# Row 35 of w2 as four eight-partition transfers in a gated attention and MLP decode step

## The chip, the cores and the metric

The kernel runs on one core of a Trainium2 chip. The metric is the device time of one execution in microseconds (us). Three runs of the kernel before gave a median of 721.89 us (721.79 to 722.36).

## The reference

All tensors are float32. Two tokens (B = 2) pass through an attention block with a cache and through an MLP, and a gate mixes the two.

```python
# D = 576, H = 32 heads, Dh = 128, Sk = 4096 cached positions, F = 4608
g = sigmoid((x * gate_w).sum(-1))                      # one gate per token
q = x @ wq                                             # [2, 32 heads, 128]
p = softmax(q . k_cache * Dh**-0.5)                    # over 4096 positions
a = (p . v_cache).reshape(2, 4096) @ wo                # wo: [4096, 576]
h = gelu(x @ w1 + b1)                                  # [2, 4608]
b = h @ w2 + b2                                        # w2: [4608, 576]
return g * a + (1 - g) * b
```

The caches hold 2 x 32 x 4096 x 128 values each, 134 MB each; w2 and wo hold 10.6 MB and 9.4 MB, wq and w1 9.4 MB and 10.6 MB. Everything is read once.

## The kernel before

**The ring.** A single tile `ring` of 128 partitions holds three slots of 64 KB per partition. At the start the slots hold wq and w1. Then come 16 items, each of four heads of one token: k of an item fills one slot, its v the next, and so on round the ring (`seq`, `load_heads`, line 130). At the end three loads called `last` bring w2 and wo (`LAST`, `load_last`, line 145). Weight rows are dealt so that partition p holds rows 36p to 36p+35 of w2 and rows 32p to 32p+31 of wo. "Row r" below means the r-th row of every partition: 128 rows of 576 values, 295 KB, over all the partitions. The three `last` loads hold 28, 28 and 12 such rows, each load cut into a few transfers.

**The queue.** All these transfers are issued by SyncE (SP), one after the other, in the order of the program. SP takes its instructions in order: one that waits holds all those behind it. The waits are not written in the kernel. The framework finds, for each transfer, which earlier instructions read or wrote the bytes that it overwrites, and puts a wait on the last of them in each engine. There are eight semaphores for SP's transfers, used in turn, so a transfer also waits for the transfer eight places ahead of it.

**Slots and their release.** The first `last` load goes into the slot of v of item 14, the second into that of k of item 15, the third into that of v of item 15. A v slot is released by the products of `av` (line 493, TensorE), a k slot by the reductions of `red` (lines 461 to 463: VectorE multiplies k by q in place at line 457, GpSimd folds a part in half, VectorE sums).

**The loop over items.** The step of item i does max and softmax of item i-1, multiplies and reduces k of item i on VectorE, then does the products with v of item i-1 on TensorE.

**The end.** After the loop, `mlp_out(0, 24)` multiplies rows 0 to 23 of w2 by h, `av(15)` follows, then normalization, interleaved with the remaining rows of w2, then rows 0 to 22 of wo into the accumulator `acc`, and rows 23 to 31 into `res` (`last_out`, line 415). The last row of wo comes in three pieces, so that little is left to do when the last one lands. `acc_mm(lhsT, rhs, k)` multiplies one row by two tokens: two products of 288 columns.

`hg` (line 384) is the gated h: hg[p, r, b] goes with row 36p + r of w2.

Of the kernel before, what the change touches and what calls it, by code (L numbers as in the profile page):

```python
# [8 lines left out]
F32 = mybir.dt.float32  # L9
AF = mybir.ActivationFunctionType  # L10
ALU = mybir.AluOpType
AX = mybir.AxisListType
P = 128
# [6 lines left out]
def kernel(  # L20
# [14 lines left out]
    nc = tc.nc  # L35
    B, H, SK, DH = k_cache.shape
    D = x.shape[-1]
# [20 lines left out]
    NF = F // P  # L58
# [5 lines left out]
    SLOTS = 3  # L64

    LAST = (
        (("w2", 0, 14), ("w2", 14, 28)),
        (("w2", 28, 36), ("wo", 0, 10), ("wo", 10, 20)),
        (("wo", 20, 23), ("wo", 23, 27), ("wo", 27, 30), ("wo", 30, 31), ("wo", 31, 32)),
    )  # L70
    FOLD = 23
    SLOT = R * DH
# [8 lines left out]
    cp = ctx.enter_context(tc.tile_pool(name="cp", bufs=1))  # L81
# [8 lines left out]
    ps_sm = ctx.enter_context(tc.tile_pool(name="ps_sm", bufs=3, space=bass.MemoryType.PSUM))  # L90
# [8 lines left out]
    kt, vt, wqt, w1t, rows = {}, {}, {}, {}, {}  # L99
# [22 lines left out]
    def slot(n):  # L122
        k = len(held) % SLOTS
        return ring[:, k * SLOT:k * SLOT + n]

    def load_heads(src, i):
# [3 lines left out]
        nc.sync.dma_start(t, src[i % B, h:h + E].rearrange("h (p r) d -> (h p) (r d)", p=PE_))  # L130
        return t.rearrange("p (r d) -> p r d", d=DH)

    srcs = {"w2": w2.rearrange("(p r) n -> p (r n)", r=NF), "wo": wo.rearrange("(p r) n -> p (r n)", r=32)}

    def load_last(m):
        n = sum(z - a for _, a, z in LAST[m]) * D

        used["e"], used["z"] = len(held) % SLOTS * SLOT + n, (len(held) % SLOTS + 1) * SLOT
        t = slot(n)
        o = 0  # L140
        for w, a, z in LAST[m]:

            ends = (a * D, a * D + DS, a * D + DS + DO, z * D) if (w, z) == ("wo", 32) else (a * D, z * D)
            for u, v in zip(ends, ends[1:]):
                nc.sync.dma_start(t[:, o:o + v - u], srcs[w][:, u:v])
                o += v - u
            for r in range(a, z):
                rows[w, r] = t[:, o - (z - r) * D:o - (z - r - 1) * D]

    def temp(n, parts=P):  # L150
        t = ring[:parts, used["t"]:used["t"] + n]
        used["t"] += n
        assert used["t"] <= SLOTS * SLOT
        return t
# [7 lines left out]
    def load():  # L162
        if not seq:
            return
        kind, i = seq.pop()
        if kind == "wq":
            wqt[i] = load_w(wq, ROWS[kind], i)
        elif kind == "w1":
            w1t[i] = load_w(w1, ROWS[kind], i)
        elif kind == "k":  # L170
            kt[i] = load_heads(k_cache, i)
        elif kind == "v":
            vt[i] = load_heads(v_cache, i)
        else:
            load_last(i)
        if kind in ("k", "v", "last"):
            held.append((kind, i))
# [28 lines left out]
    ident = cp.tile([P, P], F32, name="ident")  # L206
# [12 lines left out]
    for j in range(NPB):  # L219
        t = cp.tile([P, NT * EB + 32 - EB], F32, name=f"p{j}")  # L220
# [121 lines left out]
    def acc_mm(lhsT, rhs, k, start=False, stop=False):  # L342
        m = lhsT.shape[-1]
        for s in range(NS):
            o = 64 * (k % 2) + 32 * s
            nc.tensor.matmul(  # L346
                acc[o:o + m], lhsT, rhs[:, s * DS:(s + 1) * DS], start=start, stop=stop, skip_group_check=True
            )
# [27 lines left out]
    hg = cp.tile([P, NF, B], F32, name="hg")  # L376
    t = temp(NF * B).rearrange("p (r b) -> p r b", b=B)
# [6 lines left out]
    nc.vector.tensor_mul(hg, t, g1.unsqueeze(1).to_broadcast([P, NF, B]))  # L384
    load()

    def mlp_out(lo, hi):
        for r in range(lo, hi):
            acc_mm(hg[:, r], rows["w2", r], r)
# [6 lines left out]
    def o_turn(turn):  # L396
        t = late(B * 32).rearrange("p (b c) -> p b c", c=32)
        for b in range(B):
            nc.vector.transpose(t[:, b], oT[:, b])
        ps = ps_sm.tile([P, B * 32], F32, tag="sm", name="op_t")  # L400
        nc.tensor.matmul(ps, turn, t.rearrange("p b c -> p (b c)"), start=True, stop=True)
        nc.vector.tensor_copy(oP.rearrange("p b c -> p (b c)"), ps)

    def wo_out(lo, hi):
        for r in range(lo, hi):
            acc_mm(oP[:, :, r], rows["wo", r], r)
# [110 lines left out]
    def norm_sum():  # L517
        sums = ps_sm.tile([NO, 1], F32, tag="sm", name="psum")
        nc.tensor.matmul(sums, rs, ones, start=True, stop=True)
        f = late(1, NO)  # L520
        nc.vector.reciprocal(f, sums)
        nc.vector.tensor_mul(f, f, gall)
        nc.vector.tensor_reduce(osum, oall.rearrange("p (r d) -> p d r", d=DH), AX.X, ALU.add)
        nc.vector.tensor_scalar_mul(osum, osum, f[:, 0:1])

    def norm_t():
        ps = ps_sm.tile([P, NO], F32, tag="sm", name="oT_t")
        nc.tensor.transpose(ps, osum, ident[:NO, :NO])
        nc.vector.tensor_copy(
            oT.rearrange("p b (h e) -> p h b e", e=E), ps.rearrange("p (h b e) -> p h b e", b=B, e=E)  # L530
        )
# [22 lines left out]
    max_n(k)  # L554
    softmax(k)
    mlp_out(0, 24)
    av(k)
    load_next(("v", k))
# [4 lines left out]
    nc.vector.tensor_copy(turn.rearrange("p (h k) -> p k h", k=KB), ident.rearrange("p (k h) -> p k h", k=KB))  # L563
    osum = late(DH, NO)
    norm_sum()
    mlp_out(24, 30)
    norm_t()
    mlp_out(30, 33)
    o_turn(turn)
    mlp_out(33, 36)  # L570
    wo_out(0, FOLD)
    last_out()

# [27 lines left out]
```

## Time and profile before

| | |
|---|---|
| median of three runs | 721.89 us (721.79 to 722.36) |
| profiled execution, first to last instruction (span) | 720.1 us |
| time of the profiled execution beyond its span | not listed; 1.8 us lie between its span and the median of the runs |
| bytes read | 308.59 MB, 429 GB/s over the span |
| SP's DMA queue | 99.2% of the 16 DMA engines' span |
| VectorE (DVE) busy | 517.7 us (72%) |
| TensorE (PE) busy | 237.1 us (33%) |
| GpSimd (POOL) busy | 143.2 us (20%) |
| ScalarE (ACT) busy | 37.8 us (5%) |

The profile is one execution on the chip. "SPq" is the issue of a transfer by SP, not its run on the DMA engines. A row of the timeline gives start, duration, engine, line, operation, output and input, and in brackets how long the engine stood idle before it and what ended that. In the strips of digits a digit is the busy share of a slice in tenths.

### The profile page before, as it was taken

The numbers are of one execution on the slowest core, as the hardware profiler recorded it, in microseconds if no ns is written. First come the engines' busy times: TensorE is split into PE (matmuls) and PEld (weight loads), VectorE is DVE, ScalarE is ACT, GpSimd is POOL, SyncE is SP. The second block draws the span as 40 slices with busy tenths as digits, with TensorE's granted clock in tenths as the row PEclk, the third lists the DMA queues.
The fourth block names the chain that finished last, engine by engine and source line by source line (L and its number), as shares of the span: only waits on it lengthen the run. The fifth ranks groups of instructions, "written<-read, shape, count | busy, mean of one in ns | idle before, by whom it ended". The sixth has DMA issues, their size and how long they took to land.

```text
span 720.1 us, 3893 instructions
## 1 busy us (share of the span) xinstructions
PE 237.1 (33%) x1661; PEld 72.7 (10%) x1661; DVE 517.7 (72%) x150; ACT 37.8 (5%) x141; POOL 143.2 (20%) x28
## 2 busy tenths in 40 slices
PE   0755022140516060604142140506060503324197
PEld 0321000010101010101010000101010101001033
DVE  0004969879696969696969879696969596978900
ACT  0010010100101010101010100101010101010000
POOL 1000130404050403022040404040503113040400
PEclk9967557575757575665757575757575665757589
DMA  9999999999999999999999999999999999999997
GB/s 409 411 443 430 433 440 415 459 416 451 422 444 420 437 433 426 442 430 440 434 433 440 426 434 433 430 433 434 440 430 444 423 448 422 444 426 430 422 427 299
DMA packets 7101, 308.84 MB, mean 429 GB/s; under 512 B 798, under 2 KB 1182, under 8 KB 1580
## 3 DMA queue, kind: packets, MB, share of 16 engines
q1 hardware_dynamic: 7060, 308.55, 99.2%
q8 instruction: 13, 0.21, 0.1%
q10 hardware_dynamic: 24, 0.05, 0.0%
q14 instruction: 4, 0.03, 0.0%
HBM read 308.59 MB, written 0.00 MB: 429 GB/s over the span
## 4 chain that ended last, share of the span: by engine, by line
DMA 46%; DVE 35%; PE 17%; ACT 1%; issue 1%; POOL 0%; ACTq 0%; DVEq 0%; SPq 0%; POOLq 0%
DMA ring<-in_A_k_cache_dram 39%; DVE ring L457 19%; DVE s L462 10%; PE av L493 9%; DVE s L463 5%; DMA ring<-in_A_wo_dram 3%; DMA ring<-in_gate_w_dram 3%; PE qps L282 2%; PE hps L282 2%; PE oall L511 1%; PE acc L346 1%; PE mt L472 1%; ACT p L482 1%; DMA ring<-in_B_b_dram 1%; PE qps L307 1%
## 5 line engine op out<-in xcount | busy, mean ns | idle before, releaser
L457 DVE TENSOR_TENSOR ring<-ring,q 128x16384 f32<-128x16384 f32 x16 | 275.6, 17225 | 102.2 <-DMA ring<-in_A_k_cache_dram 102.2
L461 POOL TENSOR_TENSOR ring<-ring 128x3968 f32<-128x3968 f32 x16 | 137.1, 8566 | 487.4 <-DVE ring L457 457.3
L462 DVE TENSOR_REDUCE s<-ring 128x66 f32<-128x8448 f32 x16 | 143.3, 8953 | 1.3
L493 PE MATMUL av<-ring,p 128*32 128x512 f32 x1024 | 134.4, 684 | 11.4 <-ACT p L482 6.1
L472 PE MATMUL mt<-idsc,m 128*128 128x128 f32 x32 | 12.7, 501 | 365.9 <-DVE m L467 365.9
L463 DVE TENSOR_REDUCE s<-ring 128x62 f32<-128x3968 f32 x16 | 68.4, 4276 | 0.0
L482 ACT ACTIVATE p<-s,bs 32x128 f32<-32x128 f32 x64 | 25.5, 398 | 483.0 <-DVE bs L476 481.8
L493 PEld LDWEIGHTS av<-ring,p 128*32 128x32 f32 x1024 | 35.8, 125 | 119.6 <-issue 102.9
L472 PEld LDWEIGHTS mt<-idsc,m 128*128 128x128 f32 x32 | 8.0, 312 | 382.1 <-DVE m L467 353.5
L330 PE MATMUL qb<-qm,spread 64*128 64x512 f32 x8 | 8.3, 1137 | 69.8 <-POOL qm L326 69.8
L511 PE MATMUL oall<-avs,pick 128*64 128x512 f32 x32 | 30.6, 1059 | 0.8 <-DVE avs L505 0.8
L505 DVE TENSOR_TENSOR avs<-av,selr 128x512 f32<-128x512 f32 x16 | 10.9, 681 | 15.9 <-PE av L493 15.9
L369 DVE TENSOR_TENSOR ring<-hps,ring 128x384 f32<-128x384 f32 x3 | 1.7, 559 | 17.4 <-PE hps L282 17.3
L240 DVE COPY ring<-ring 3x64 f32<-3x64 f32 x2 | 0.3, 182 | 19.0 <-DMA ring<-in_gate_w_dram 19.0
L326 POOL TENSOR_TENSOR qm<-qall,mine 64x512 f32<-64x512 f32 x4 | 4.1, 1034 | 46.2 <-ACT qall L309 46.2
L301 DVE COPY ring<-ident 128x8 f32<-128x8 f32 x8 | 0.7, 169 | 16.9 <-DMA ring<-in_B_b_dram 16.9
L482 ACT ACTIVATION_READ_ACCUMULATOR p<-s,bs 32x1 f32 x64 | 11.8, 184 | 0.0
L282 PE MATMUL qps<-ring 128*32 128x512 f32 x80 | 11.6, 746 | 0.0
L282 PE MATMUL hps<-ring 128*32 128x384 f32 x120 | 11.5, 547 | 0.0
L346 PE MATMUL acc<-ring,hg 128*2 128x288 f32 x144 | 11.4, 453 | 0.0
L437 DVE COPY ring<-res 2x144 f32<-2x144 f32 x2 | 0.6, 300 | 12.7 <-PE res L415 12.7
L330 PEld LDWEIGHTS qb<-qm,spread 64*128 64x128 f32 x8 | 2.0, 307 | 72.9 <-POOL qm L326 72.9
(80 smaller groups left out, 75.2 us busy)
## 6 DMA issues: line engine op xcount, KB each, us to landing
ring<-in_B_w_dram SPq DMA_DIRECT2D x2, 4608.0 KB, 34.5
ring<-in_B_w_dram SPq DMA_DIRECT2D x2, 4032.0 KB
ring<-in_A_wo_dram SPq DMA_DIRECT2D x2, 2880.0 KB, 19.3
ring<-in_B_w_dram SPq DMA_DIRECT2D x1, 2304.0 KB, 13.3
ring<-in_A_wo_dram SPq DMA_DIRECT2D x2, 864.0 KB
ring<-in_B_w_dram SPq DMA_DIRECT2D x1, 1152.0 KB
ring<-in_A_wo_dram SPq DMA_DIRECT2D x1, 1152.0 KB
ring<-in_A_wq_dram SPq DMA_DIRECT2D x1, 1024.0 KB, 24.1
```

Source lines behind the costliest of these rows:

```text
L282: nc.tensor.matmul(ps[32 * j:32 * j + 32, :width], lhs, ts[c][:, o:o + width], start=(k == 0), stop=last, skip_group_check=True,)
L330: nc.tensor.matmul(ps, spread, t.rearrange("p u d -> p (u d)"), start=True, stop=True)
L346: nc.tensor.matmul(acc[o:o + m], lhsT, rhs[:, s * DS:(s + 1) * DS], start=start, stop=stop, skip_group_check=True)
L457: nc.vector.tensor_mul(kt[i], kt[i], qs[i].unsqueeze(1).to_broadcast([P, R, DH]))
L461: nc.gpsimd.tensor_add(t[:, :, :DH2], t[:, :, :DH2], t[:, :, DH2:])
L462: nc.vector.tensor_reduce(st[i][:, HALVED:], kt[i][:, HALVED:], AX.X, ALU.add)
L463: nc.vector.tensor_reduce(st[i][:, :HALVED], t[:, :, :DH2], AX.X, ALU.add)
L472: nc.tensor.matmul(mt[i], mx[i].to_broadcast([P, P]), idsc, start=True, stop=True)
L482: nc.scalar.activation(p[w, :, e * RB:(e + 1) * RB], st[i][w].rearrange("p (t c) -> p t c", c=RB), AF.Exp, bias=bias[i][w, e:e + 1], scale ...
L493: nc.tensor.matmul(ps[32 * j:32 * j + 32], p[:, EB * t:EB * t + 32], vt[i][:, RB * t:RB * (t + 1)].rearrange("p r d -> p (r d)"), start=(t ...
L505: nc.vector.tensor_mul(t, avs[i].rearrange("p (r d) -> p r d", d=DH), selr.unsqueeze(2).to_broadcast([P, RB, DH]))
L511: nc.tensor.matmul(oall, pick[:, NO - E - i * E:2 * NO - E - i * E], avs[i].rearrange("p r d -> p (r d)"), start=(i == 0), stop=(i == N - ...
```

## The change

Row 35 of w2 no longer comes with the other rows over 128 partitions. It comes in four transfers to partitions 0 to 31: transfer c (0 to 3) fills the eight partitions c, c+4, ..., c+28, with four runs of 576 values each. Partition 4e + c then holds row 35 of what were partitions 16e + 4c to 16e + 4c + 3. These four transfers stand in the first `last` load between rows 0 to 13 and rows 14 to 23 of w2. The three loads now bring 14 + 1 + 10 = 25, 28 and 15 rows' worth of bytes, 68 as before; in the ring, row 35 takes the room of four rows, since it fills only 32 partitions.

To multiply by it, h of row 35 is regrouped once, after `hg` is made: two reductions of the identity give a mask `mod4` (p mod 4) and a sum matrix `div4` (p div 4), a product spreads h of row 35 by p mod 4, a matmul with `div4` brings it to 32 partitions, and a copy stores it as `hx`. `mlp_x()` then makes four `acc_mm` calls on 32 partitions in place of one on 128; it stands behind `norm_sum()`.

```diff
     LAST = (
-        (("w2", 0, 14), ("w2", 14, 28)),
-        (("w2", 28, 36), ("wo", 0, 10), ("wo", 10, 20)),
-        (("wo", 20, 23), ("wo", 23, 27), ("wo", 27, 30), ("wo", 30, 31), ("wo", 31, 32)),
+        (("w2", 0, 14), ("wx", 0, 4), ("w2", 14, 24)),
+        (("w2", 24, 35), ("wo", 0, 9), ("wo", 9, 17)),
+        (("wo", 17, 23), ("wo", 23, 27), ("wo", 27, 30), ("wo", 30, 31), ("wo", 31, 32)),
     )
...
+    NR = NF - 1
+    srcx2 = w2.rearrange("(e c s r) n -> c r e s n", e=8, c=4, s=4)[:, NR]
...
         for w, a, z in LAST[m]:
+            if w == "wx":
+                x2 = t[:32, o:o + z * D]
+                rows[w] = x2
+                o += z * D
+                for c in range(4):
+                    nc.sync.dma_start(x2[c::4].rearrange("e (s n) -> e s n", s=4), srcx2[c])
+                continue
...
+    mod4 = cp.tile([P, 4], F32, name="mod4")
+    nc.vector.tensor_reduce(mod4, ident.rearrange("p (q s) -> p s q", s=4), AX.X, ALU.add)
+    div4 = cp.tile([P, 32], F32, name="div4")
+    nc.vector.tensor_reduce(div4, ident.rearrange("p (q s) -> p q s", s=4), AX.X, ALU.add)
+    hm = cp.tile([P, 4, B], F32, name="hm")
+    nc.vector.tensor_mul(
+        hm, hg[:, NR:].to_broadcast([P, 4, B]), mod4.unsqueeze(2).to_broadcast([P, 4, B])
+    )
+    hxps = ps_sm.tile([32, 4 * B], F32, tag="sm", name="hxps")
+    nc.tensor.matmul(hxps, div4, hm.rearrange("p s b -> p (s b)"), start=True, stop=True)
+    hx = cp.tile([32, 4, B], F32, name="hx")
+    nc.vector.tensor_copy(hx.rearrange("p s b -> p (s b)"), hxps)
+
+    def mlp_x():
+        for s in range(4):
+            acc_mm(hx[:, s], rows["wx"][:, s * D:(s + 1) * D], s)
...
     norm_sum()
-    mlp_out(24, 30)
+    mlp_x()
+    mlp_out(24, 29)
     norm_t()
-    mlp_out(30, 33)
+    mlp_out(29, 32)
     o_turn(turn)
-    mlp_out(33, 36)
+    mlp_out(32, NR)
     wo_out(0, FOLD)
     last_out()
```

## The prediction

> **What bounds the kernel now.** I read the page first: its DMA strip, the queues and the chain.
>
> ```profile
> span 720.1 us, 3893 instructions
> DMA  9999999999999999999999999999999999999997
> q1 hardware_dynamic: 7060, 308.55, 99.2%
> DMA 46%; DVE 35%; PE 17%; ACT 1%; issue 1%; POOL 0%; ACTq 0%; DVEq 0%; SPq 0%; POOLq 0%
> ```
>
> The chain gives VectorE 35%, but the 16 DMA engines never stand still: q1, SP's queue, fills 99.2% of them. The chain goes from an issue to the landing and does not see that the transfer stood behind others for most of that time. So the time is the bytes, as long as SP issues each transfer before the queue runs out. The question is how far ahead SP is at the place of the change. Timeline, SP's own part:
>
> ```profile
> 643.30 0.33 SPq L130 DMA_DIRECT2D ring<-in_A_v_cache_dram  x1
> 652.33 0.33 SPq L145 DMA_DIRECT2D ring<-in_B_w_dram  x1
> 655.76 0.33 SPq L145 DMA_DIRECT2D ring<-in_B_w_dram  x1
> 681.89 0.33 SPq L145 DMA_DIRECT2D ring<-in_B_w_dram  x1
> 682.64 0.80 SPq L145 DMA_DIRECT2D ring<-in_A_wo_dram  x2
> ```
>
> These are v of item 15, rows 0-13 of w2, rows 14-27, rows 28-35, and the first two pieces of wo. Between the third and the fourth lie 26 us, and the list of SP's waits says for what:
>
> ```profile
> SPq L145 <- DVE m L467: 26.0, 1, 26.0
> ```
>
> It is the release of the slot of k of item 15. VectorE's timeline shows its work on that slot (the wait is for the last sum, which ends at 677.59 + 4.28 = 681.87; the view names the instruction that begins there):
>
> ```profile
> 651.39 17.23 DVE L457 TENSOR_TENSOR ring<-ring,q 128x16384 f32<-128x16384 f32 x1 [6.62 <-DMA ring<-in_A_k_cache_dram]
> 677.59 4.28 DVE L463 TENSOR_REDUCE s<-ring 128x62 f32<-128x3968 f32 x1
> 681.90 0.29 DVE L467 TENSOR_REDUCE m<-s 128x1 f32<-128x128 f32 x1
> ```
>
> Before, this wait costs nothing, since 28 rows of w2 were already queued. How long they last needs the rate, from the DMA counts of the stretches 30 to 560 us and 560 to 715 us, and the moment at which rows 14-27 had landed, from TensorE's wait for them:
>
> ```profile
> DMA packets 4183, 230.07 MB, mean 434 GB/s; under 512 B 469, under 2 KB 469, under 8 KB 474
> q8 instruction: 8, 0.13, 0.1%
> DMA packets 2339, 66.48 MB, mean 429 GB/s; under 512 B 260, under 2 KB 505, under 8 KB 855
> q8 instruction: 4, 0.07, 0.2%
> 689.76 2.05 PEld L346 LDWEIGHTS acc<-ring,hg 128*2 128x2 f32 x40 [0.42 <-DMA ring<-in_B_w_dram]
> ```
>
> A row is 128 x 2304 = 294,912 bytes; at 429 GB/s it takes 0.687 us. Rows 14-27 landed at about 689.7, so rows 0-13 at 689.7 - 14 x 0.687 = 680.1 us. Forward it agrees: k of item 15 has landed by 651.4, v of item 15 (8.39 MB at 434 GB/s) 19.3 us later, then 14 x 0.687 = 9.6, together 680.3. With both pieces queued, SP had 689.7 - 681.9 = 7.8 us to spare. Without rows 14-27 it would be 1.8 us late. The end:
>
> ```profile
> DMA  4999989979998795874644332922222222222100
> GB/s 184 484 392 369 495 328 375 392 300 444 346 357 300 259 392 167 311 277 173 242 156 150 138 115 109 285 92 92 92 92 104 92 92 81 92 87 92 52 23 0
> 715.74 1.95 PE L415 MATMUL res<-ring,oP 128*2 128x144 f32 x40 [0.66 <-DMA ring<-in_A_wo_dram]
> 718.02 0.33 SPq L438 DMA_DIRECT2D out_dram<-ring  x1
> ```
>
> The strip covers 713 to 717 us in slices of 0.1. For its last 1.2 us a quarter of the engines (digit 2, four of 16) still works; the last byte of wo lands at 716.9, the end of the last slice that moves anything, and from there to the end of the span are 3.2 us of products, copies and the store.
>
> **The change part by part.**
>
> *The waits.* SP's list in the built program (no time in it), first of before, then of the changed kernel:
>
> ```text
> L145 DMACopy ring<-in_B_w_dram 128x8064 [waits PE_49]
> L145 DMACopy ring<-in_B_w_dram 128x4608 [waits DMAHW1_49,DVE_49]
> ---
> L149 DMACopy ring<-in_B_w_dram 8x4x576 [waits DVE_49,PE_49]
> L149 DMACopy ring<-in_B_w_dram 8x4x576 x3
> L154 DMACopy ring<-in_B_w_dram 128x5760 [waits PE_49]
> L154 DMACopy ring<-in_B_w_dram 128x6336 [waits DMAHW1_49]
> ```
>
> The wait for VectorE has moved. It stood at the first transfer into k's slot; now it stands at the first transfer of row 35, into v's slot, and its count is the one that the last sum of k of item 15 raises. These destinations step over four partitions; presumably the framework takes them for a larger region that reaches into the next slot. Whatever the reason, SP stops there until 681.87, and behind it stand the three other transfers of row 35, rows 14-23 and all of `wo`. The queue then holds v of item 15 and rows 0-13 alone and runs dry at 680.1.
>
> *The pause.* From 681.89 SP issues four transfers of row 35 ahead of rows 14-23. Two in a row took 0.80 (the wo row above), so 4 x 0.40 = 1.6 and rows 14-23 are issued at 683.5. From an issue to bytes after an empty queue, two places show: the start of the span and the store at the end (strips of 0 to 4 us and 717 to 721 us, slices of 0.1):
>
> ```profile
> 0.74 0.86 SPq L119 DMA_DIRECT2D ring<-in_A_wq_dram  x2
> DMA  0000000000000000099990900000000000000000
> GB/s 0 0 0 0 0 0 0 0 0 0 0 0 0 0 0 0 0 3277 1966 2621 1311 0 1311 0 0 0 0 0 0 0 0 0 0 0 0 0 0 0 0 0
> GB/s 0 0 0 0 0 0 0 0 0 0 0 0 0 0 0 0 0 23 23 0 0 0 0 0 0 0 0 0 0 0 0 0 0 0 0 0 0 0 0 0
> ```
>
> Issue at 0.74, bytes from slice 17, 1.7: 1.0 us. Issue at 718.02, bytes at 718.7: 0.7. Bounds 0.7 and 1.0; I take 1.0, a load like ours. So rows 14-23 flow from 684.5. [...]
>
> *Row 35 itself.* 295 KB in four transfers, issued 0.4 us apart. If each runs on eight engines, an engine gets 4 x 9216 bytes, 36.9 KB at 434/16 = 27.1 GB/s: 1.4 us, inside the 1.6 us of issues. On four engines it would be 2.7 us (1.1 more); on all 16, 0.7. I take nothing.
>
> *The rest of the bytes.* Behind it 10 + 28 + 15 = 53 rows, 53 x 0.687 = 36.4 us: to 720.9. The pause lets all engines start level again; what then separates them is the instruction blocks, 16 KB each on one engine (q8; three of them from 690 to 720 us):
>
> ```profile
> q8 instruction: 3, 0.05, 0.6%
> ```
>
> 16,384 bytes at 27.1 GB/s are 0.6 us on the engine that gets one. The last byte lands at 721.5, where it was 716.9: **+4.6 us**.
>
> *The slots behind it.* Rows 14-23 land at 684.5 + 6.9 = 691.4, where rows 14-27 had at 689.7. So TensorE's `mlp_out` and the products of item 15 slide by 1.7 us, and with them the release of the third load:
>
> ```profile
> 695.00 20.69 DMA ring<-in_A_wo_dram
> 708.87 3.56 PE L346 MATMUL acc<-ring,oP 128*2 128x288 f32 x52 [0.98 <-DMA ring<-in_A_wo_dram]
> ```
>
> Its issue at about 695 becomes 696.7; the second load lasts until 691.4 + 28 x 0.687 = 710.6. It is 14 us early: no second pause.
>
> *`mlp_x`.* Eight products for two, each in two passes. 52 passes took 3.56 us, 0.07 each: 12 more are 0.8 us, before TensorE's wait for `wo`, which shows it has time. Afterwards a row of `wo` takes four passes, 0.3 us, against 0.69 for its bytes. Nothing.
>
> *The preparation.* Four VectorE instructions and a matmul ahead of the first multiplication:
>
> ```profile
> 70.44 17.22 DVE L457 TENSOR_TENSOR ring<-ring,q 128x16384 f32<-128x16384 f32 x1 [0.61 <-DMA ring<-in_A_k_cache_dram]
> 102.05 0.29 DVE L476 TENSOR_REDUCE bs<-mt 128x4 f32<-128x128 f32 x1 [0.89 <-PE mt L472]
> 109.12 17.22 DVE L457 TENSOR_TENSOR ring<-ring,q 128x16384 f32<-128x16384 f32 x1 [6.78 <-DMA ring<-in_A_k_cache_dram]
> ```
>
> Two reductions and two small ones at 0.29 at most, with a matmul in between that takes 0.89 to come back: 2.1 us. 0.61 is idle; 1.5 us are late, and the next item's wait of 6.78 takes them up. Nothing at the end; without that cover it would be 1.5.
>
> **Sum.** +4.6 us on a span of 720.1: 724.7. The median lies 1.8 us above this span, which is outside it and unchanged: 721.89 + 4.6 = **726.5 us**.
>
> **The rivals.**
>
> *No pause, and a little faster.* The wait ends early, row 35 and rows 14-23 are queued at 655.8, the queue never empties. It decides itself at 680.1 minus 0.7 to 1.0: if rows 14-23 are issued by 679, this holds. Then only the shares of the engines change. If row 35 leaves the engines that finish last (the four of the strip), 18.4 KB at 27.1 GB/s come off them: -0.7 us, 721.2. If it goes onto them, +0.7, 722.6. [...] Against this rival: SP's 26.0 us wait and its new place. Chance 0.05.
>
> *A shorter pause.* Bytes flow 0.7 after the issue, no instruction block falls on the last engine, the rows go at 434 GB/s (0.68): 684.2 + 53 x 0.68 = 720.2, +3.3, 725.2. Chance 0.2, that it comes nearer to this than to my sum.
>
> *A longer one.* The issues of row 35 take more than 0.40 each, since each serves half of the engines, or run on four engines (1.1), or the first packets after the pause are slow. 1.5 us more: 728.0. Chance 0.2.
>
> My sum has 0.55.
>
> **How the numbers follow.** 726.5 is the likeliest. The range takes in the short and the long pause, 725.2 to 728.0, and leaves out the rival without one and what lies beyond. 0.2% of this kernel, 1.4 us, is about what a measurement can tell from no change. Slower is the sum and both pauses, 0.95; without a pause the result is within 0.2% either way, 0.04; 0.01 is left for a gain.
>
> **What the profile of the changed kernel would show.** SP's wait of about 26 us for VectorE ends at the first transfer of row 35, at 681.9, and nothing of w2 is issued between 652.3 and then. The DMA strip has a hole from about 680 to 684. TensorE waits for rows 14-23 until about 691.4. The span grows by about as much as the hole. I am wrong if SP issues row 35 near 655, or if the strip is full and the time is still longer.

## The result, and the profile after

The changed kernel takes 731.24 us (median; 731.1 to 731.4) against 721.84 for the kernel before: 1.0128 of its time, with a 95% interval of 1.0116 to 1.014. It is slower by 9.4 us, where 4.6 were forecast, and lies outside the range of 725.2 to 728.0.

The page of the changed kernel, then SP's waits and SP's part of its timeline:

```profile
span 729.1 us, 3934 instructions
DMA  9999999999999999999999999999999999999597
q1 hardware_dynamic: 7220, 308.55, 98.1%
```

```profile
SPq L149 <- DVE s L489: 29.2, 1, 29.2
```

```profile
652.14 0.33 SPq L154 DMA_DIRECT2D ring<-in_B_w_dram  x1
681.77 3.45 SPq L149 DMA_DIRECT2D ring<-in_B_w_dram  x4
685.28 1.02 SPq L154 DMA_DIRECT2D ring<-in_B_w_dram  x2
686.35 23.51 SPq L154 DMA_DIRECT2D ring<-in_A_wo_dram  x9
```

The bytes are the same 308.55 MB, but the strip, full before, has a 5 near its end. SP waits 29.2 us for VectorE's last sum of k of item 15, now at the first transfer of row 35 (line 149). Between rows 0-13 at 652.14 and that transfer at 681.77 it issues nothing. The four transfers take 3.45 us of SP's time, and rows 14-23 are issued at 685.28 only. The DMA strip from 676 to 700 us (slices of 0.6) shows the hole, TensorE's wait its other edge:

```profile
DMA  7821100000002232299199799879969949779889
```

```profile
694.87 4.09 PE L355 MATMUL acc<-ring,hg 128*2 128x288 f32 x40 [5.15 <-DMA ring<-in_B_w_dram]
```

The queue runs dry between 676.5 and 679.7, as each engine ends. From 683.4 row 35 trickles through (the digits 2 and 3); each of its four transfers has eight completions in the packet records, where one over 128 partitions has 16. The strip is full again only from about 686.5. Rows 14-23 have landed by 694.5.

### The profile page after: what moved, and what is told of

It reads as the page before. It is cut to its first block, busy times and chain, and to the rows that moved or that the text cites. A ratio compares the mean times of both kernels' runs of the same rounds, so it can differ in the third digit from the quotient of the medians.

```text
span 729.1 us, 3934 instructions
## 1 busy us (share of the span) xinstructions
PE 238.7 (33%) x1675; PEld 73.3 (10%) x1675; DVE 518.3 (71%) x154; ACT 37.9 (5%) x141; POOL 143.3 (20%) x28
## 3 DMA queue, kind: packets, MB, share of 16 engines
q1 hardware_dynamic: 7220, 308.55, 98.1%
## 4 chain that ended last, share of the span: by engine, by line
DMA 47%; DVE 34%; PE 16%; issue 1%; ACT 1%; SPq 0%; POOL 0%; ACTq 0%; DVEq 0%; POOLq 0%
DMA ring<-in_A_k_cache_dram 39%; DVE ring L483 19%; DVE s L488 10%; PE av L519 9%; DVE s L489 5%; DMA ring<-in_A_wo_dram 3%; DMA ring<-in_gate_w_dram 3%; PE hps L291 2%; PE qps L291 2%; DMA ring<-in_B_w_dram 1%; PE oall L537 1%; DMA ring<-in_B_b_dram 1%; ACT p L508 1%; PE mt L498 1%; PE acc L355 1%
## 5 line engine op out<-in xcount | busy, mean ns | idle before, releaser
L355 PE MATMUL acc<-ring,hg 128*2 128x288 f32 x140 | 13.0, 504 | 5.1 <-DMA ring<-in_B_w_dram 5.1
```

Source lines behind the costliest of these rows:

```text
L355: nc.tensor.matmul(acc[o:o + m], lhsT, rhs[:, s * DS:(s + 1) * DS], start=start, stop=stop, skip_group_check=True)
```

## The experiments

All are compared with the kernel before, run beside them. "The last byte" is the end of the last packet of wo in the trace's packet records: 716.9 us in the kernel before, 725.6 in the changed kernel.

### Row 35 without the early wait

The first question was whether the loss is the pause at all, or the new transfers themselves. Transfer c goes to neighbouring partitions; in the built program the wait then stands again at rows 24-34.

```diff
-    nc.sync.dma_start(x2[c::4].rearrange("e (s n) -> e s n", s=4), srcx2[c])
+    nc.sync.dma_start(x2[8 * c:8 * c + 8].rearrange("e (s n) -> e s n", s=4), srcx2[c])
...
-    nc.vector.tensor_reduce(div4, ident.rearrange("p (q s) -> p q s", s=4), AX.X, ALU.add)
+    nc.vector.tensor_reduce(div4, ident.rearrange("p (e c s) -> p c e s", c=4, s=4), AX.X, ALU.add)
```

> The changed kernel, but transfer c of row 35 fills the eight neighbouring partitions 8c to 8c+7 instead of c, c+4, ..., c+28, and the sum matrix has its columns in the same order. In the built program the wait for VectorE is back at rows 24-34 of w2. Pause theory: the queue never runs dry, and the time is that of before less at most the share of row 35 that leaves the late engines: 721.2, and 722.6 if it goes onto them. Rival (the transfers of row 35 cost by themselves, wherever they stand: 3.5 us of SP's time for four issues, short runs on eight engines): 724 or more.

Measured: 723.06 us (722.8 to 724.99), 1.0024 of before (1.0013 to 1.0035). SP's wait in the profile stands at line 154 again:

```profile
SPq L154 <- DVE m L493: 25.6, 1, 25.6
```

Eight of the 9.4 us are gone, with the preparation, `mlp_x` and four small transfers still in place. But it is not the gain that was expected: the last byte lands at 717.4, 0.5 after that of before. The median lies between the two forecasts, and three of the seven runs are above 724. So something in these transfers costs too, though little.

The same with the strided partitions of the change, at a place where SP waits in any case:

```diff
-        (("w2", 0, 14), ("wx", 0, 4), ("w2", 14, 24)),
-        (("w2", 24, 35), ("wo", 0, 9), ("wo", 9, 17)),
+        (("w2", 0, 14), ("w2", 14, 28)),
+        (("w2", 28, 35), ("wx", 0, 4), ("wo", 0, 9), ("wo", 9, 17)),
```

> The changed kernel with its strided partitions, but the four transfers of row 35 stand in the second load, right behind rows 28-34 of w2, where SP has waited for VectorE in any case. Pause theory: no hole, 721.2 as with neighbouring partitions (0.7 under before), since rows 0-27 are queued when SP waits. Rival that strided partitions are slow in themselves: above the kernel with neighbouring partitions by more than 0.2%.

Measured: median 723.05 us, with five runs at 721.81 to 722.11 and six at 723.05 to 723.25, ratio 1.0009 (1.0 to 1.0018). That is above the 721.2 expected. SP's timeline and wait of this kernel:

```profile
651.55 30.60 SPq L154 DMA_DIRECT2D ring<-in_B_w_dram  x3
682.58 3.02 SPq L149 DMA_DIRECT2D ring<-in_B_w_dram  x4
```

```profile
SPq L154 <- DVE m L493: 26.8, 1, 26.8
```

The issues of row 35 are as slow as in the changed kernel, 3.02 us for four, and the wait is 26.8 us long. Here neither costs anything, since rows 0-27 are queued. The last byte of the profiled execution lands at 716.4, 0.5 before that of the kernel before, near the 0.7 expected. That gain doesn't reach the time: 3.5 us lie between the last byte and the end of the span (3.2 before), and the profiled run took 2.2 us beyond its span. All runs of the kernels with row 35 apart took 2.0 to 2.3 us beyond their spans, those without it 1.7 to 1.9; where this comes from is not shown. Seen once more:

> The kernel with row 35 in the second load, strided partitions, once more, to see the upper of the two times that it takes (five runs at 721.8 to 722.1, six at 723.1 to 723.3). At the lower one the last byte landed at 716.4. If it shows the upper one, the last byte should land at about 717.6, by one instruction block (1.4 us) more on an engine that ends late; or the bytes land at 716.4 and the rest is later.

Measured: 722.93 us, one run. The last byte lands at 717.2, between the two times forecast, and one engine alone is late. DMA throughput from 713 to 718 us in slices of 0.125, of this execution:

```profile
GB/s 355 392 415 373 392 304 396 318 355 314 300 341 313 249 249 343 194 235 152 180 134 138 88 55 60 32 18 28 28 18 23 23 18 9 0 0 0 0 0 0
```

The row of 18 to 28 GB/s is one engine's rate (434/16 = 27). Why one engine is late in some executions and not in others stays open. This kernel does not beat the one before, and its fastest run (721.81) is the fastest of all those with row 35 apart.

In one transfer to 32 partitions:

```diff
-                for c in range(4):
-                    nc.sync.dma_start(x2[c::4].rearrange("e (s n) -> e s n", s=4), srcx2[c])
+                nc.sync.dma_start(
+                    x2.rearrange("q (s n) -> q s n", s=4),
+                    w2.rearrange("(q s r) n -> q r s n", s=4, r=NF)[:, NR],
+                )
```

> Row 35 in one transfer to partitions 0 to 31, four runs each, in place of four transfers of eight partitions. No early wait for VectorE. If it spreads over all 16 engines, each engine has the bytes it had before: 721.9, as before. [...] SP's issue should take about 0.4 us, if the 0.7 to 0.9 of the changed kernel belongs to transfers on eight engines.

Measured: 723.98 us, 1.0029 (1.0018 to 1.0041), above the expectation. It uses all 16 engines (16 completions in the packet records), but the last byte lands at 718.9, 2.0 later than before; why is not shown. SP's one issue takes 0.70 us, not 0.4, so a slow issue does not need a transfer on eight engines.

Neighbouring and strided partitions at one place, the second load:

> Row 35 in the second load, behind rows 28-34, as in the kernel with that place and strided partitions (whose last byte landed at 716.4, before 716.9), but to neighbouring partitions 8c to 8c+7. [...] If the partitions don't matter, the two kernels agree.

Measured: 723.44 us (722.64 to 725.69), 1.0025 (1.0015 to 1.0036). The last byte lands at 717.5; the two profiled executions of the strided version at the same place had 716.4 and 717.2. The last byte depends on one engine, so the stream as a whole tells more. In the packet records the packets of rows 28-34, ahead of row 35, end at the same time in all three executions, 690.1 to 690.2 on the mean. Those of rows 0-8 of wo, behind it, end at 696.55 and 696.50 with strided partitions and at 697.47 with neighbouring ones. SP's issues go the other way:

```profile
682.34 1.36 SPq L149 DMA_DIRECT2D ring<-in_B_w_dram  x4
```

Four in 1.36 us with neighbouring partitions, 3.02 with strided ones at the same place. So, here, strided partitions cost SP 1.7 us and save the stream 0.9 to 1.0.

### The early wait without row 35

Rows 14-27 behind the first transfer of the second load, in the kernel before:

```diff
+    if (w, a) == ("w2", 14):
+        used["put"] = t[:, o:o + v - u], srcs[w][:, u:v]
+    else:
+        nc.sync.dma_start(t[:, o:o + v - u], srcs[w][:, u:v])
+    if (w, a) == ("w2", 28):
+        nc.sync.dma_start(*used["put"])
-    nc.sync.dma_start(t[:, o:o + v - u], srcs[w][:, u:v])
```

> The kernel before, with rows 14-27 of w2 issued behind rows 28-35, and so behind the wait for VectorE. Nothing of row 35 is changed. It is the pause without the four slow issues. Issue at 681.9, bytes 1.25 us later (as in the changed kernel's trace), 54 rows at 0.687 us, one instruction block of 1.4 us on the last engine: last byte at 721.6 against 716.9, so 721.9 + 4.7 = 726.6. If the whole loss of 9.4 us is the pause, it comes out near 731; then the slow issues cost nothing.

Measured: 729.9 us, 1.0112 (1.0097 to 1.0128). The last byte lands at 721.9, within 0.3 of the forecast, but 6.1 us follow it instead of 3.2. TensorE's timeline says why:

```profile
699.53 4.71 PE L351 MATMUL acc<-ring,hg 128*2 128x288 f32 x40 [10.34 <-DMA ring<-in_B_w_dram]
716.93 5.75 PE L351 MATMUL acc<-ring,oP 128*2 128x288 f32 x90
```

Rows 14-27 now land behind rows 28-35, all of item 15's products slide with them, and TensorE goes through the rows of `wo` without a wait (90 products in one row of the view, with no idle time ahead of them): it is the bound at the end. So this run has two effects and doesn't price the pause alone.

A cleaner form leaves the order as it was. Rows 14-27 come in four transfers of 32 partitions, written as two runs each:

```diff
+    if (w, a) == ("w2", 14):
+        for c in range(4):
+            nc.sync.dma_start(
+                t[c::4, o:o + v - u].rearrange("p (s n) -> p s n", s=2),
+                srcs[w][c::4, u:v].rearrange("p (s n) -> p s n", s=2),
+            )
+    else:
+        nc.sync.dma_start(t[:, o:o + v - u], srcs[w][:, u:v])
-    nc.sync.dma_start(t[:, o:o + v - u], srcs[w][:, u:v])
```

> The kernel before, with rows 14-27 of w2 in four transfers, each to every fourth partition (c, c+4, ..., 32 partitions) and written as two runs per partition, so that the wait for VectorE stands at them in the built program, as in the changed kernel. Row 35 is not touched. It is the early wait without small transfers: the first of the four brings bytes for 2.4 us, so the other issues are hidden. Issue at 681.9, bytes 1.25 us later, 54 rows at 0.687 us, 1.4 us for an instruction block on the last engine: last byte at 721.7 against 716.9, 726.7 in all. The part of the 9.4 us above that belongs to the issues of row 35. If the wait alone makes the whole loss: 731.

Measured: 728.08 us (727.5 to 729.24), 1.0089 (1.0072 to 1.0106): 6.2 us above before. The last byte lands at 722.9, 1.2 after the forecast, and the time is 1.4 above it. Its counterpart writes each as one run, `t[c::4, o:o + v - u]` from `srcs[w][c::4, u:v]`:

> The kernel before, with rows 14-27 of w2 in four transfers to every fourth partition, as in the kernel of the same form that lost 6.2 us, but written as one run per partition. The built program's transfers are the same four; only the wait for VectorE stands again at rows 28-35. If the early wait is the cause, the loss goes: 721.9, within 0.3. If transfers to every fourth partition are slow, the 6.2 us stay, about 728.

Measured: 722.07 us (721.93 to 722.41), 1.0003 (0.9993 to 1.0013), the same as before. The built program of both has the same four transfers of 32 x 8064 elements; only the place of the wait differs. SP's timeline and wait with two runs written, then the same two views with one:

```profile
652.51 0.33 SPq L152 DMA_DIRECT2D ring<-in_B_w_dram  x1
681.63 2.75 SPq L147 DMA_DIRECT2D ring<-in_B_w_dram  x4
```

```profile
SPq L147 <- DVE s L470: 28.7, 1, 28.7
```

```profile
651.89 0.33 SPq L149 DMA_DIRECT2D ring<-in_B_w_dram  x1
655.33 2.74 SPq L147 DMA_DIRECT2D ring<-in_B_w_dram  x4
```

```profile
SPq L149 <- DVE m L471: 23.6, 1, 23.6
```

The four issues take the same 2.74 us and stand 26.3 us apart. In the packet records, the packets of rows 14-27 end 6.0 us later on the mean with two runs written than with one (689.28 and 683.28). The early wait alone costs 6 us of the 9.4, and it comes from the form in which the destination is written: a step over partitions together with a split into runs. The step alone does not bring it (here), nor does the split alone (neighbouring partitions).

### The issues of row 35 on an empty queue

In the changed kernel, with the wait where it is, one transfer of row 35 stays ahead of rows 14-23 and three follow:

```diff
-                for c in range(4):
-                    nc.sync.dma_start(x2[c::4].rearrange("e (s n) -> e s n", s=4), srcx2[c])
+                nc.sync.dma_start(x2[0::4].rearrange("e (s n) -> e s n", s=4), srcx2[0])
                 continue
...
+            if (w, a) == ("w2", 14):
+                for c in range(1, 4):
+                    nc.sync.dma_start(x2[c::4].rearrange("e (s n) -> e s n", s=4), srcx2[c])
```

> The changed kernel, with only the first of the four transfers of row 35 ahead of rows 14-23 and the other three right behind them. The wait stays where it is. If the issues of row 35 ahead of rows 14-23 cost time while the queue is empty, rows 14-23 are issued 2.6 us earlier (682.7 for 685.3), and with row 35's bytes then in the stream of the lower engines the last byte lands at 721.8 for 725.6: 727.4. If these issues cost nothing: 731.

Measured: 728.39 us, 1.0094 (1.0079 to 1.0109), 2.9 under the changed kernel. SP's timeline:

```profile
682.03 0.85 SPq L148 DMA_DIRECT2D ring<-in_B_w_dram  x1
682.93 0.40 SPq L153 DMA_DIRECT2D ring<-in_B_w_dram  x1
683.77 2.15 SPq L157 DMA_DIRECT2D ring<-in_B_w_dram  x3
```

This is 1.0 above the forecast of 727.4. Rows 14-23 are issued at 682.93 instead of 685.28, 2.4 us earlier. The packets of rows 0-8 of wo end 1.95 us earlier on the mean (703.29 for 705.24): the 2.4 less about 0.5 for the three quarters of row 35 (0.75 x 0.687) that now flow behind rows 14-23. The last byte, on one engine, comes 2.9 earlier; what gives it the remaining 0.9 is not shown. So on the empty queue the three issues ahead of the large transfer cost their time, 2.4 us. That row 35 lies on the lower engines, as the forecast of 727.4 has it, no run shows: the packet records of the changed kernel have eight completions for each of its four transfers and no names of engines.

Row 35 behind rows 14-23, still in the first load:

```diff
-        (("w2", 0, 14), ("wx", 0, 4), ("w2", 14, 24)),
+        (("w2", 0, 14), ("w2", 14, 24), ("wx", 0, 4)),
```

> The changed kernel with row 35 behind rows 14-23 in the first load. The wait for VectorE stands at row 35, but rows 14-23 are queued ahead of it and last until 683.5 on the first engine and 686.7 on the last. Row 35 and rows 24-34 are issued from 681.8 to 685.3 and flow from 686.5. Pause theory: a hole of up to 3 us on the early engines and almost none on the late ones; last byte about 1 us later than before, 722 to 723.5. If the place of row 35 in front of the second load costs anything of its own: 725 or more.

Measured: 724.29 us, 1.0032 (1.0019 to 1.0046), 0.8 above the expected stretch and under the 725 of the rival; the last byte lands at 718.7, 1.8 after that of the kernel before, where 1 was forecast. DMA strip from 676 to 700 us:

```profile
DMA  9799989989988844596193995995959998899889
```

What was a hole of fifteen slices is a dent of a few. SP still waits 26.2 us for VectorE at row 35; how much is queued ahead of the wait makes 7 us of difference.

## Why the prediction was right in sign and wrong in size

**The moved wait: right.** SP stops at the first transfer of row 35 until 681.8, for the sum named, with rows 14-23 and everything else behind it. The wait is 29.2 us rather than 26, since it begins as soon as rows 0-13 are issued at 652.14. The counterparts with one run and two (722.07 and 728.08) show that the place of the wait alone does it. The reason given, that the framework takes the destination for a larger region, was only presumed; the runs show which form brings the wait, not what the framework does inside.

**The dry queue at 680.1: right.** The last engine ends rows 0-13 at 679.7; 14 of the 16 have ended by 678.5.

**The issues of row 35, 1.6 us: wrong.** This term was taken from two issues of wo, of 128 partitions, at 0.40 each. The four took 3.5 us, and rows 14-23 were issued at 685.28, not 683.5: 1.8 us. The run with one transfer ahead shows that this time is lost to the stream.

**From the issue to bytes, 1.0 us: too small.** Ten rows take 6.87 us, and the first engine had its share of rows 14-23 at 693.96; counted back, it ran at full rate from 687.1, 1.8 after the issue, and the last engine from 687.6. In the run with four transfers of 32 partitions it is about 1.95 after the first issue. The start of the span shows when the first packet begins, not when the stream runs full. Here the first packet of rows 14-23 begins at 686.53, 1.25 after the issue, near the forecast; but the first packet of each engine takes 0.9 to 1.95 us, where later ones of the same size take 0.86. Together that is 0.8 to 1.3 us more than forecast.

**The instruction block, 0.6 us: too small.** It was priced by its bytes. In the packet records of the changed kernel 15 engines have their share of rows 24-34 by 702.0, and the one that got the block at 698.7 at 702.9; from its place before, 1.4 us late. The block itself takes 0.92 us, and the packet behind it 1.45 instead of 0.94. The engine that ends last is the one that got the next block, at 715.3. From 694.5 to the last byte at 725.6 are 31.1 us, where 43 rows and a block had been put at 30.1: 1.0 us, of which the block makes 0.8.

**The end: slightly too small.** 3.5 us from the last byte to the end of the span for 3.2, and 731.24 - 729.1 = 2.1 beyond the span for 1.8: 0.6 us.

Together 1.8 + 1.3 + 1.0 + 0.6 = 4.7: 726.5 + 4.7 = 731.2. All four terms belong to the restart of an empty queue or to what follows it, and all erred to one side. The rival of a longer pause named both of the large ones, slow issues and slow first packets, and gave them 1.5 us in all. Its reason for the slow issues, that each serves half of the engines, does not hold: with neighbouring partitions four such issues took 1.36 us in one kernel and 1.69 in another, 0.34 and 0.42 each.

**No second pause, `mlp_x`, the preparation: right.** TensorE waits for `wo` again at the end (719.74 and later), and the kernel with all of these and no pause takes 721.8 to 722.1 in five of its eleven runs. The preparation was put at 1.5 us late and cost less still: VectorE begins the first multiplication at 70.63 instead of 70.44.

**The rival without a pause** would not have been as good as it was priced either: the last byte gains 0.5 in one execution with row 35 in the second load and loses 0.3 in the other, it loses 0.5 with neighbouring partitions, and the time gains in none.

## What to carry to other kernels

Before timing a change to a transfer, list what each transfer waits for in the built program: here, a destination that steps over partitions and is split into runs got a wait for a slot that it doesn't touch (28.7 and 29.2 us), and the queue behind it paid (728.08 us against 722.07). When SP's queue empties, the price is not the gap alone: in this kernel three issues ahead of the next large transfer held it back by 2.4 us, and from its issue to a full stream it took 1.8 to 2.3 us more. Let a large transfer stand first behind a long wait, and small ones behind it (728.39 us with three of the four behind it, against 731.24), or put them where a queue of several transfers covers them (723.05).

## What the runs showed of the hardware that was not expected

- **An issue's cost differed with the destination.** In the second load, where the queue does not run dry, four eight-partition transfers took SP 1.36 us to neighbouring partitions and 3.02 to every fourth one.
- **Partitions that lie together slowed the bytes here.** With row 35 to neighbouring partitions the packets behind it end 0.9 to 1.0 us later than with every fourth one, and one transfer to 32 partitions brings the last byte 2.0 later than the row over 128. The runs don't show why.
- **An instruction block of 16 KB delayed its DMA engine by about 1.4 us** (0.92 for the block, 0.51 for the packet behind it), more than twice the 0.6 us of its bytes at 27.1 GB/s. In the kernel before, the four engines that end last (716.7 to 716.9, against 713.8 to 715.5) are those that got two of the 13 blocks before their last byte. On this kernel, bound by its queue (99.2% before, 98.1% after), that sets which engine ends last.
